# Fused attention and feed-forward kernel: other slots for the loads and turns of the tenth head pair

## The chip, the cores and the metric

The kernel runs on one core of one Trainium2 chip. The metric is the device time of one execution in microseconds (us), lower is better. The kernel before took 505.3 us, the median of 3 runs (504.86, 505.3 and 510.37).

An engine here is one of the core's instruction streams: PE (matrix products), PEld (PE's weight loads, which overlap PE), DVE (vector work), ACT (functions such as exp and tanh), POOL (general work), SP (issues transfers). Each works through its own list in order. ACT and SP also issue the DMA transfers of this kernel.

## The reference

There are 8 batches of 8 heads, sequence 576, head dimension 64. For every head, scores are formed, all that lie more than tau below the row's maximum are dropped, and the rest goes through a softmax; then a feed-forward layer with g = h - tanh(h) works on the 4608 rows of 512:

```
scores = scale * np.matmul(q, k.transpose(0, 1, 3, 2))
thresh = np.max(scores, axis=-1, keepdims=True) - tau
scores = np.where(scores >= thresh, scores, -1000000000.0)
scores = scores - np.max(scores, axis=-1, keepdims=True)
attn = np.exp(scores)
attn = attn / (np.sum(attn, axis=-1, keepdims=True) + 1e-09)
out = np.matmul(attn, v)
...
h = x @ w_in
g = h - np.tanh(h)
return (g @ w_out).astype(np.float32)
```

## The kernel before

**Tiles and slots.** Two heads make a pair; there are 32 pairs, numbered from 0, so that the tenth is pair 9. A pair has nine tiles of 128 query rows (four for each head, and one that holds the last 64 rows of both), 288 tiles in all. One loop runs over slots, one tile per slot. In slot s it issues, in this order: the scores of tile s+8 (PE, L401 and L410, reduced to a maximum by DVE in L420), the thresholding of tile s+5 (ACT, L447, which writes z), the feed-forward work that is due (PE L579 and L605, ACT L592, DVE L598), the exponentials (ACT L483, from the transposed z), the product with v of tile s-2 (PE L506, L513, L524), and at the end of the slot the steps that a plan has for it. After these come casts of the feed-forward weights (POOL, L731) and loads of further pieces of them (SP, L739, up to slot 53), at slots that two lists give.

**Who transposes z.** From pair 6 on, z is turned by a DMA transpose that SP issues (L454, zT), one for two tiles; before that PE turns it. Exponentials of two tiles are then one activation, in every second slot.

**What a pair needs before its scores.** Pair p's first scores are issued at slot 9p-8, which the code calls `first`: 73 for pair 9, 64 for pair 8, 82 for pair 10. For the pairs from 8 on (`DUAL`) eleven steps lead up to that, each with a lead d: the step is issued at the end of slot first-d.

- `k0`, `q0`, `q1`, `v0`, `v1`: loads of raw float32 data, issued by ACT (L175). k comes in one transfer of 288 KB, q in one of 256 KB and one of 32 KB, v in two, of 128 KB and 160 KB.
- `ks`, `qs`, `vs`: POOL splits k and q into a high and a low float16 half (L228, L231, L232; three passes each) and casts v to bfloat16 into one of four vb buffers (L261, L265, L266).
- `kt`, `qt`: SP issues a DMA transpose of the split k or q (L315), which gives kT and qT. For k of pair 8 PE does it.
- `kw`: POOL copies kT with its two halves exchanged (L337), which gives kS.

Raw and split data have two buffers per kind, kT, kS and qT three. `FIRST_LATER` has leads of their own for pairs 8 and 9, `LATER` has those of the later pairs, by even and odd number; pair 9's in the kernel before are the same as `LATER[1]`. The order of the list matters for steps of one slot alone. Within one slot, a pair with a lower number goes first. Since each engine takes its instructions in order, a lead sets both the time from which a step may run and what stands ahead of it in ACT's, POOL's or SP's queue.

Of the kernel before, what the change touches and what calls it, by code (L numbers as in the profile page):

```python
# [18 lines left out]
def kernel(  # L19
# [713 lines left out]
    def w_load(piece):  # L733
# [6 lines left out]
        else:  # L740
# [35 lines left out]
            ("kw", 3),  # L776
        ),
        9: (
            ("kt", 10), ("qt", 6), ("k0", 18), ("q0", 14), ("v0", 15),
            ("q1", 13), ("v1", 12), ("ks", 11), ("qs", 8), ("vs", 6),  # L780
            ("kw", 5),
        ),
    }
    for p in range(DUAL, NPAIR):
# [176 lines left out]
```

## Time and profile before

| what | value |
|---|---|
| median of 3 runs | 505.3 us |
| the profiled execution | 511.62 us, its span 509.7 us |
| PE busy | 484.8 us (95% of the span) |
| ACT busy | 431.7 us (85%) |
| DVE busy | 400.2 us (79%) |
| POOL busy | 291.4 us (57%) |
| transfers issued by SP | 75.1% of 16 DMA engines over the span |
| transfers issued by ACT | 16.1% |
| zT, issue to landing | median 4.7 us |
| kT, qT, issue to landing | median 5.2 and 4.3 us |
| k load issued by ACT, issue to landing | median 4.2 us |

The page of the profile describes one execution, which was 6.3 us longer than the median. Its second part cuts the span into 40 equal slices of about 12.7 us and gives a digit, in tenths, for each engine's busy share, for the clock granted to PE and for the DMA engines' share. An answer by stages gives the same for chosen stretches. A timeline lists instructions with start, duration and, in brackets, the idle time of the engine before them with what ended it. The time that a DMA issue takes on its queue is not the time that its data takes to land.

In this execution pair 9's loads went out at 88.87 us (k), 92.65 (v0), 97.67 (q0, and q1 behind it) and 100.77 (v1).

### The profile page before, as it was taken

What the parts mean: (1) busy time and instruction counts of PE and PEld (TensorE: products, weight loads), DVE (VectorE), ACT (ScalarE), POOL (GpSimd) and SP (SyncE); (2) the same over time, 40 slices, a digit from 0 to 9 for tenths busy, and PEclk for the clock granted to TensorE, in tenths of its full rate; (3) what the DMA queues carried; (4) which work ended last, traced back from release to release, by engine and by line L of the source; (5) the groups of instructions that cost most, each with busy time, mean ns of one, the idle gap of its engine ahead of it and who ended that gap; (6) DMA issues with size and microseconds to landing.
All of it is one profiled execution on the core that took longest, in us unless ns stands there. A gap on an engine that the chain in (4) does not pass through costs nothing.

```text
span 509.7 us, 12184 instructions
## 1 busy us (share of the span) xinstructions
PE 484.8 (95%) x4283; PEld 270.9 (53%) x4345; DVE 400.2 (79%) x1150; ACT 431.7 (85%) x617; POOL 291.4 (57%) x390
## 2 busy tenths in 40 slices
PE   8999899889999989999999999999998999999997
PEld 4666566445555545555555555555554555544444
DVE  5899978878889879988898789889886887544440
ACT  5999998889999889999999999899979999533430
POOL 8999999886765375757675666569456700000000
PEclk9999999989999999999999999999999999999999
DMA  7852658999999999999999999999999986311013
GB/s 206 262 155 89 195 190 220 159 225 214 231 217 245 192 254 209 238 241 242 242 195 221 261 238 225 207 242 240 213 191 258 187 144 115 87 41 42 23 41 82
DMA packets 233341, 95.32 MB, mean 187 GB/s; under 512 B 203968, under 2 KB 222656, under 8 KB 233280
## 3 DMA queue, kind: packets, MB, share of 16 engines
q1 hardware_dynamic: 212336, 72.87, 75.1%
q10 hardware_dynamic: 20944, 21.67, 16.1%
q8 instruction: 34, 0.56, 0.5%
q14 instruction: 27, 0.22, 0.2%
HBM read 36.70 MB, written 9.44 MB: 91 GB/s over the span
## 4 chain that ended last, share of the span: by engine, by line
PE 57%; POOL 12%; DMA 9%; issue 7%; ACT 7%; DVE 5%; ACTq 1%; SPq 0%; POOLq 0%; DVEq 0%
PE psY L605 18%; PE psH L579 14%; PE psS L410 13%; DMA zT<-z 6%; PE psO L513 3%; POOL kS L337 3%; PE psHt L579 3%; ACT pT L483 3%; DMA vraw<-in_v_dram 3%; ACT z L447 2%; DVE g L598 2%; POOL qhl L232 2%; DVE sc L420 2%; PE psS L401 2%; ACTq L175 1%
## 5 line engine op out<-in xcount | busy, mean ns | idle before, releaser
L420 DVE TENSOR_SCALAR_CACHE_REDUCE sc<-psS 128x576 f32<-128x576 f32 x288 | 213.5, 752 | 27.1 <-PE psS L410 12.9
L447 ACT ACTIVATE z<-sc,nb 128x576 bf16<-128x576 f32 x288 | 216.1, 770 | 8.0 <-DVE nb L432 5.7
L483 ACT ACTIVATE pT<-zT 128x1152 f16<-128x1152 bf16 x117 | 135.2, 1155 | 12.3 <-DMA zT<-z 10.6
L605 PE MATMUL psY<-w_out_sb,g 128*128 128x512 bf16 (+1 forms) x564 | 140.8, 373 | 1.6 <-issue 0.2
L579 PE MATMUL psH<-xT,w_in_sb 128*128 128x512 bf16 x448 | 119.4, 381 | 5.1 <-issue 2.0
L337 POOL COPY kS<-kT 64x1152 f16<-64x1152 f16 x62 | 70.8, 1142 | 86.3 <-DMA kT<-khl 72.7
L598 DVE SCALAR_TENSOR_TENSOR g<-th,psH 128x512 bf16<-128x512 f32 x128 | 87.6, 685 | 33.6 <-ACT th L592 32.9
L410 PE MATMUL psS<-kT,qT 128*128 128x512 f16 (+1 forms) x512 | 104.7, 286 | 4.1 <-DVE sc L420 1.9
L410 PE MATMUL psS<-kS,qT 128*128 128x512 f16 (+1 forms) x512 | 105.1, 287 | 0.0
L410 PEld LDWEIGHTS <-qT 128*128 128x128 f16 x1024 | 72.5, 98 | 59.0 <-issue 3.8
L592 ACT ACTIVATE th<-psH 128x512 f32<-128x512 f32 x128 | 74.6, 583 | 21.4 <-PE psH L579 21.4
L605 PEld LDWEIGHTS <-g 128*128 128x128 bf16 x592 | 51.1, 98 | 54.6 <-DVE g L598 0.4
L579 PEld LDWEIGHTS <-w_in_sb 128*128 128x128 bf16 x576 | 49.4, 98 | 57.4 <-issue 6.3
L513 PE MATMUL psO<-vb,pT 128*128 128x65 bf16 x1024 | 53.3, 194 | 0.0
L513 PEld LDWEIGHTS <-pT 128*128 128x128 f16 x1024 | 44.2, 98 | 9.6
L232 POOL TENSOR_TENSOR qhl<-qraw,qhl 128x576 f16<-128x576 f32 x31 | 39.7, 1281 | 2.6
L232 POOL TENSOR_TENSOR khl<-kraw,khl 128x576 f16<-128x576 f32 x31 | 39.7, 1280 | 2.7
L475 ACT ACTIVATE pT<-psZ 128x512 f16<-128x512 bf16 (+1 forms) x54 | 35.1, 654 | 2.4 <-PE psZ L466 2.1
L506 PE MATMUL psO<-vb,pT 128*128 128x130 bf16 x128 | 28.2, 220 | 3.7 <-ACT pT L483 3.6
L617 DVE COPY yo<-psY 128x512 f32<-128x512 f32 (+1 forms) x31 | 21.1, 680 | 13.1 <-PE psY L605 12.4
L539 DVE TENSOR_TENSOR osb<-psO,rc 128x256 bf16<-128x256 f32 x64 | 27.2, 424 | 2.2
L228 POOL TENSOR_SCALAR qraw<-qraw 128x576 f32<-128x576 f32 x31 | 20.8, 671 | 11.1 <-DMA qraw<-in_q_dram 10.8
(77 smaller groups left out, 452.1 us busy)
## 6 DMA issues: line engine op xcount, KB each, us to landing
out_dram<-yo SPq DMA_DIRECT2D x32, 256.0 KB, 3.8
kraw<-in_k_dram ACTq DMA_DIRECT2D x24, 288.0 KB, 4.2
qraw<-in_q_dram ACTq DMA_DIRECT2D x24, 256.0 KB, 4.3
wt<-in_moe_w_in_dram SPq DMA_DIRECT2D x8, 512.0 KB, 4.6
wt<-in_moe_w_out_dram SPq DMA_DIRECT2D x8, 512.0 KB, 3.9
vraw<-in_v_dram ACTq DMA_DIRECT2D x24, 160.0 KB, 4.3
vraw<-in_v_dram ACTq DMA_DIRECT2D x24, 128.0 KB, 3.8
vraw<-in_v_dram SPq DMA_DIRECT2D x8, 256.0 KB, 3.6
```

Of the source, the lines that this page charges most:

```text
L232: nc.gpsimd.tensor_tensor(out=hl[:, :, 1, :], in0=x, in1=hl[:, :, 0, :], op=ALU.subtract)
L337: nc.gpsimd.tensor_copy(out=o, in_=i)
L410: nc.tensor.matmul(out=ps[:, dst], lhsT=lhs, rhs=cols(p, kk, hh), start=(n == 0), stop=(n == 1),)
L420: nc.vector.tensor_scalar(out=sc, in0=ps[:, lo : lo + S], scalar1=SC, scalar2=None, op0=ALU.mult, op1=ALU.max, accum_out=mx[:, c : c + 1],)
L447: nc.scalar.activation(out=z, in_=sc, func=ACT.Prelu, bias=nb, scale=1.0, alpha=STEEP)
L475: nc.scalar.activation(out=pt[:, off * P : (off + n) * P], in_=ps[:, 0 : n * P], func=ACT.Exp)
L483: nc.scalar.activation(out=pt[:, 0 : n * P], in_=zts.pop(i)[:, 0:n, :], func=ACT.Exp)
L513: nc.tensor.matmul(out=po[:, t - 1 + ab, :], lhsT=pt[:, blk * P : (blk + 1) * P], rhs=vb[:, hh, c, :], start=False, stop=(n == 7), skip_gr ...
L579: nc.tensor.matmul(out=ps, lhsT=w_in_sb[:, c, n * P : (n + 1) * P], rhs=xs[m][:, c, :] if m < B else xR[:, c, :, :], start=(c == 0), stop= ...
L592: nc.scalar.activation(out=th, in_=ps, func=ACT.Tanh)
L598: nc.vector.scalar_tensor_tensor(out=gs[m][:, n, :], in0=th, scalar=-1.0, in1=ps, op0=ALU.mult, op1=ALU.add,)
L605: nc.tensor.matmul(out=ps, lhsT=gs[m][:, n, ms * P : (ms + 1) * P], rhs=w_out_sb[:, n, cols], start=(n == 0), stop=(n == DF_C - 1),)
```

## The change

Pair 9 gets another list. Nine of its eleven steps move; nothing is added or removed, and no other pair is touched.

| step | queue | slot before | slot after |
|---|---|---|---|
| k0 | ACT | 55 | 52 |
| q0 | ACT | 59 | 55 |
| q1 | ACT | 60 | 56 |
| v0 | ACT | 58 | 57 |
| v1 | ACT | 61 | 59 |
| ks | POOL | 62 | 60 |
| qs | POOL | 65 | 62 |
| kt | SP | 63 | 63 |
| qt | SP | 67 | 65 |
| kw | POOL | 68 | 66 |
| vs | POOL | 67 | 67 |

Pair 8's own steps lie at 46 (k0), 49 (q0, q1), 50 (v0), 52 (v1), 54 (qs), 56 (ks), 57 (kt), 58 (vs) and 59 (qt); pair 10's begin with k0 at 64.

```diff
         9: (
-            ("kt", 10), ("qt", 6), ("k0", 18), ("q0", 14), ("v0", 15),
-            ("q1", 13), ("v1", 12), ("ks", 11), ("qs", 8), ("vs", 6),
-            ("kw", 5),
+            ("k0", 21), ("v1", 14), ("q0", 18), ("v0", 16), ("qs", 11),
+            ("q1", 17), ("qt", 8), ("ks", 13), ("vs", 6), ("kt", 10),
+            ("kw", 7),
         ),
```

## The prediction

> **What bounds the kernel now.** I read the page first: span, busy shares, slices.
>
> ```profile
> span 509.7 us, 12184 instructions
> ...
> PE 484.8 (95%) x4283; PEld 270.9 (53%) x4345; DVE 400.2 (79%) x1150; ACT 431.7 (85%) x617; POOL 291.4 (57%) x390
> ...
> PEclk9999999989999999999999999999999999999999
> DMA  7852658999999999999999999999999986311013
> ```
>
> PE is busy 95% of the span, so a moved load is worth only what PE stands still for it. Two things stand out: the DMA share goes to 9 from the eighth slice on (about 89 us), where the zT transposes have begun, and the clock row has one 8, in the ninth slice (102 to 115 us). Pair 9 (the tenth) is loaded just before. So next comes the table by stage, core 0 (the stretch and its length; busy us and count of PE, PEld, DVE, ACT, POOL; then clock, DMA share, GB/s):
>
> ```profile
> 84.00:88.00 4.00, 3.88 (x43) 2.49 (x44) 3.28 (x11) 3.90 (x8) 3.73 (x7) 1.00 1.01 241
> 88.00:92.00 4.00, 3.60 (x39) 1.93 (x37) 3.92 (x13) 3.57 (x6) 3.85 (x5) 1.00 1.31 201
> 92.00:96.00 4.00, 3.95 (x49) 2.66 (x48) 4.00 (x13) 3.84 (x6) 2.08 (x3) 1.00 1.09 99
> 96.00:100.00 4.00, 2.73 (x27) 1.41 (x25) 3.02 (x10) 2.33 (x3) 3.76 (x6) 1.00 1.46 186
> 100.00:104.00 4.00, 1.69 (x17) 0.72 (x15) 2.27 (x7) 3.88 (x6) 3.85 (x5) 1.00 1.06 225
> ...
> 104.00:108.00 4.00, 3.77 (x17) 1.88 (x19) 1.76 (x4) 3.41 (x6) 3.75 (x7) 0.57 1.36 235
> ```
>
> At 92 to 96 the DMA engines are full and yet move 99 GB/s, where the stages around move 186 to 241. Right after it PE falls to 2.73 and 1.69 of 4 us. The timeline of PE, ACT and SP says why (start, us, instruction; in brackets the idle time before it and what ended it):
>
> ```profile
> 98.88 0.23 PE L506 MATMUL psO<-vb,pT 128*128 128x130 bf16 x1 [1.27 <-ACT pT L483]
> 101.98 0.23 PE L506 MATMUL psO<-vb,pT 128*128 128x130 bf16 x1 [0.77 <-ACT pT L483]
> 104.02 0.42 PE L410 MATMUL psS<-kT,qT 128*128 128x512 f16 x2 [1.55 <-DMA qT<-qhl]
> ```
> ```profile
> 92.65 0.61 ACTq L175 DMA_DIRECT2D vraw<-in_v_dram  x1
> 97.67 1.16 ACT L483 ACTIVATE pT<-zT 128x1152 f16<-128x1152 bf16 x1 [1.83 <-DMA zT<-z]
> 97.67 1.06 ACTq L175 DMA_DIRECT2D qraw<-in_q_dram  x2
> ```
> ```profile
> 87.87 9.58 SPq L454 DMA_TRANSPOSE zT<-z  x3
> 97.63 2.04 SPq L315 DMA_TRANSPOSE qT<-qhl  x1
> ```
>
> The exponentials wait for a zT, PE for the exponentials, and last for pair 8's qT, issued behind three zTs and beside pair 9's two q loads at 97.67. The chain of work that ended last runs through the same place (start, us, what):
>
> ```profile
> 91.28 9.46 DMA zT<-z
> 100.74 0.02 issue
> 100.76 0.01 ACT pT L483
> 100.77 4.70 DMA vraw<-in_v_dram
> ```
>  The three waits are 1.27+0.77+1.55 = 3.6 us. At clock 0.57 a busy 3.77 us does the work of 0.57×3.77, so 1.6 us more goes. The stretch costs **5.2 us**.
>
> **What the Trainium skill says.** "DMA: Bandwidth & Descriptors", section "Issuing engines are not separate DMA queues": transfers started by ACT and SP run on the same 16 engines and interleave. The trace agrees: pair 9's k load (ACT, 88.87) took 8.6 us to land, the slowest of the two zTs (SP) issued from 87.5 to 92 took 9.8, against a zT median of 4.7. "Perfetto Trace Analysis", section on HWDGE DMA instructions: an issue's duration is lock wait plus descriptor generation, and the data movement is outside it. The trace agrees: zT issues at 84.76, 87.87 and 94.14 took 1.26, 2.01 and 3.31 us, their landings more. "TensorE: Matmul & The Clock Gate", Part 1: idle PE drops to half clock, in windows of 3.4 us. Here 0.57 over 4 us fits one such window (1-0.5×3.4/4 = 0.575).
>
> **The change part by part.** No instruction or byte is added; eleven steps keep their kind, nine change slot. One slot is about 1.4 us here (nine tiles in 13.4).
>
> *k0 from slot 55 to 52 (ACT queue).* It will go out behind v1 of pair 8, which is in slot 52 already (84.62, 0.65 us), so at about 85.3 instead of 88.87. Its 0.35 us issue then is in the open: the activation over it is 0.60 long, v1 alone uses that up, so ACT is later by up to 0.4. ACT had a hole of 0.43 at 88.3 (z waits for th) that takes it: 0. Buffer: pair 7's k was split by POOL at 74.74 to 77.5; no wait. Its 288 KB are 1.4 us of DMA time at the 206 GB/s of 86 to 92, so the zT at 84.76 (landed 89.17, used at 92.30: cover 3.1) lands up to 1.4 later: 0.
>
> *q0 59 to 55, q1 60 to 56, v0 58 to 57, v1 61 to 59 (ACT queue).* q0 takes k0's place at 88.9 (256 KB for 288), q1 (32 KB) follows at about 91, v0 moves from 92.65 to about 92.3, v1 from 100.77 to 97.67. Issues of 0.40, 0.59, 0.61, 0.61 us lie under activations of 0.57 to 1.16: 0. The two q loads leave 97.67, where they share the engines with qT of pair 8: 288 KB or 1.4 us of DMA time go from there, v1's 160 KB come. The zTs at 87.87 and 91.28 get q0, q1 for k0: bytes equal within 10%, smaller rows. The zT at 87.87 was wanted at 95.84, when ACT fell idle: 8.0 us after issue, against 4.4 for the zT before it, a cover of 3.6.
>
> *ks 62 to 60, qs 65 to 62 (POOL queue).* The three-pass splits are 2.7 us each (0.67+0.66+1.28 with gaps). ks passes one weight cast (1.04), so starts at 99.35 instead of 100.36; qs 103.06 instead of 104.07. Its loads land by 97. The cast of slot 60 ends at about 103.1 instead of 100.4; the first psY matmul is at 115.3: cover 12. 0.
>
> *kt stays at 63, qt 67 to 65 (SP queue).* qt now stands ahead of the zT of slot 66, behind that of slot 64, whose issue ends at 108.7; qhl is ready at 105.8. The zT of slot 66 goes from 109.05 to about 110.0, lands at 113.8 instead of 112.76; its exponential is at 116.84. Cover 3: 0. qT of pair 9 comes 1.8 earlier, wanted by PE at 117.25: 0.
>
> *kw 68 to 66, past vs (POOL queue).* POOL's swap waits for kT (issued 104.07, landed 109.66, as SP holds kt at its place); vs (1.3 us) now waits behind it, to 113.4 instead of 108.07. Pair 9's vb is first read in slot 85, after 134: cover 20. Pair 10's ks, qs start 1.3 later (113.4, 116.1); its kt goes out at 116.81 and needs ks by then (116.1): cover 0.7, and if that went, the swap (120.6) would slip against a first use at 130: 0.
>
> So all moved issues cost nothing under these covers; what is left is **the stretch of 5.2 us**. Bounds: all of it goes, if the 99 GB/s stage needs k0 beside the zTs of 87.87 and 91.28; none, if q0 in its place does the same; and as much again is lost (+5.2) in an execution without it, if k0 and v1 together do it one zT earlier.
>
> What is in the runs that set the median? The profiled execution took 511.62 us (span 509.7 and 1.9 around it), the median is 505.3, 6.3 less; the runs are 504.86, 505.3 and 510.37. Taking the stretch out of the profiled time gives 506.4, near the median. I take it that the median's execution has most of it not: zTs land in the ordinary 4.4. Then the third zT issue ends at 94.14+1.3 = 95.4, qT of pair 8 goes at 95.6 and lands 4.3 later (page median of qT) at 99.9; PE, without 2.04 of earlier waits, wants it at 102.47-2.04 = 100.4. That cover is 0.5, and one pressed landing (1.4 of DMA time by the q loads) makes a wait of 0.9. The change removes the q loads from beside it: between 0 and 1.4; I take 0.7. **505.3-0.7 = 504.6**. For an execution with the stretch: 511.6-5.2 = 506.4.
>
> **The rivals.** *A, forecast*: covers hold, only the thin cover at qT matters: 503.9 to 505.3, with run spread 503 to 506.5. For: every cover above. Against: the median may carry the stretch. Chance 0.52. *B, faster*: all executions carry the stretch, so all lose it: 505.3-5.2 = 500.1. For: the load that landed in 8.6 us is the very one moved. Against: 506.4 would be what is left of the profile, and pairs 10 to 31 also have k0 beside transposes, and later PE stands still for over 1 us only near 180 and 380. Chance 0.14, nearly all of it over 1%. *C, slower*: at slot 52, k0 follows the zT of 84.76 by 0.55 us with v1 (160 KB) and a 512 KB weight piece in flight. k loads at 263.35 and 370.77, out 0.6 and 0.55 us after a zT, landed in 6.6 and 6.8. If zTs at 84.76 and 87.87 then land over 7.5 us after issue (the covers of 7.5 and 8.0 decide), PE pays 3.6 waiting and a half-clock window, 5.2: 510.5. Chance 0.19. *D, it does not matter*: the stretch comes as before, only with q0: the time stays at 505.3 to 505.8. Chance 0.15; it falls within 1%.
>
> **Numbers.** A measurement of this kernel tells about 1% (5 us) from no change. Within 1%: A 0.52, D 0.15 and the part of B and C that is milder, 0.05: 0.72. Slower 0.17, faster 0.11. The range reaches to B and C's centres, 500.1 and 510.5, and leaves out about half of each, under 0.2: 500.0 to 510.6. A alone spans 503 to 506.5.
>
> **What would show it.** Right: k landing in under 6 us from 85.3, no stage at 88 to 100 below 150 GB/s, qT of pair 8 landing before PE asks, no 8 in the clock row. If C: waits for zT already at 92 to 96. If the thin cover is nothing: qT's wait gone and the time still 505.3. Wrong altogether: a wait of PE or POOL at 116 to 135 on pair 9's or 10's tiles, which would show one of the covers false.

## The result, and the profile after

The changed kernel takes 512.28 us (median of 17 runs, 509.41 to 519.67), the kernel before in the same comparison 507.56 (17 runs, 503.42 to 514.73). The ratio is 1.0107, 95% interval 1.0079 to 1.0136: slower by about 1%. The ratios here leave out the runs that took over 1.5% more than the fastest of the same kernel, the medians do not, and since this kernel scatters by more than that the two can differ by half a per cent. The median of before is 2.3 us above the 505.3 of the three runs that the prediction had.

The profiled execution of the changed kernel took 513.09 us. From the first and second part of its page:

```profile
span 511.2 us, 12245 instructions
...
PE 490.9 (96%) x4345; PEld 271.1 (53%) x4345; DVE 399.2 (78%) x1150; ACT 431.4 (84%) x617; POOL 291.8 (57%) x390
...
PEclk9999999999999999999999999999999999999999
DMA  7852657999999999999999999999999876311013
```

The 8 in the clock row is gone. (The profile of before, and every other of a whole kernel here, records 62 matrix products fewer, x4283 against x4345, so the busy times of PE over the span are not comparable.) The table by stage of the changed kernel, with the same columns as in the prediction:

```profile
88.00:92.00 4.00, 3.70 (x39) 1.89 (x36) 3.64 (x12) 4.00 (x7) 3.85 (x5) 1.00 1.11 279
92.00:96.00 4.00, 3.93 (x48) 2.54 (x47) 4.00 (x12) 3.83 (x6) 1.79 (x2) 1.00 1.23 162
96.00:100.00 4.00, 3.62 (x35) 1.85 (x32) 3.84 (x12) 3.66 (x6) 3.70 (x7) 1.00 1.26 225
100.00:104.00 4.00, 3.47 (x32) 1.93 (x31) 2.63 (x9) 4.00 (x6) 3.85 (x5) 1.00 1.23 237
104.00:108.00 4.00, 3.17 (x36) 1.92 (x34) 3.78 (x11) 3.89 (x7) 3.12 (x4) 1.00 1.29 139
```

Nothing here falls to 99 GB/s, and PE is busy for 3.17 us of 4 or more, where before had a stage with 1.69. Read against the first profile alone, this stretch is better: the score reduction (DVE, L420) of tile 72, pair 8's first, starts at 102.7 us, where it was 105.0. (Below, a tile's start is the start of its score reduction.) A second profile of the kernel before settles which of the two is the ordinary case. Its rows, same columns:

```profile
92.00:96.00 4.00, 3.95 (x49) 2.66 (x48) 4.00 (x13) 4.00 (x7) 2.08 (x3) 1.00 1.08 256
96.00:100.00 4.00, 3.62 (x30) 1.81 (x28) 3.96 (x13) 3.81 (x6) 3.77 (x6) 1.00 1.17 196
100.00:104.00 4.00, 3.68 (x32) 2.06 (x32) 2.46 (x8) 4.00 (x7) 3.85 (x5) 1.00 1.14 152
```

256 GB/s at 92 to 96, full clock, and tile 72 at 101.8. So the stretch is not in every execution; of the eight profiles with pair 9's k and q at their old places or later (below), the first alone has it. Against the second profile the changed kernel is late at each step: tile 72 (pair 8's first) by 0.9 us, tile 81 (pair 9's) by 1.8, tile 90 (pair 10's) by 3.0.

### The profile page after: what moved, and what is told of

It reads as the page before. It is cut to its first block, busy times and chain, and to the rows that moved or that the text cites. A ratio compares the mean times of both kernels' runs of the same rounds, so it can differ in the third digit from the quotient of the medians.

```text
span 511.2 us, 12245 instructions
## 1 busy us (share of the span) xinstructions
PE 490.9 (96%) x4345; PEld 271.1 (53%) x4345; DVE 399.2 (78%) x1150; ACT 431.4 (84%) x617; POOL 291.8 (57%) x390
## 4 chain that ended last, share of the span: by engine, by line
PE 57%; DMA 11%; POOL 11%; ACT 9%; issue 5%; DVE 3%; ACTq 2%; SPq 0%; POOLq 0%
PE psY L605 18%; PE psH L579 15%; PE psS L410 13%; DMA zT<-z 10%; ACT z L447 4%; ACT pT L483 4%; PE psO L513 3%; PE psHt L579 3%; POOL kS L337 2%; ACT th L592 2%; PE psS L401 2%; ACTq L175 2%; DVE g L598 1%; PE psO L524 1%; DVE sc L420 1%
## 5 line engine op out<-in xcount | busy, mean ns | idle before, releaser
L420 DVE TENSOR_SCALAR_CACHE_REDUCE sc<-psS 128x576 f32<-128x576 f32 x288 | 213.2, 751 | 22.3 <-PE psS L410 12.5
L483 ACT ACTIVATE pT<-zT 128x1152 f16<-128x1152 bf16 x117 | 135.2, 1156 | 15.2 <-DMA zT<-z 13.3
L605 PE MATMUL psY<-w_out_sb,g 128*128 128x512 bf16 (+1 forms) x592 | 145.7, 373 | 0.0
L579 PE MATMUL psH<-xT,w_in_sb 128*128 128x512 bf16 x480 | 123.3, 379 | 2.0 <-DVE g L598 1.8
L410 PE MATMUL psS<-kT,qT 128*128 128x512 f16 (+1 forms) x512 | 104.4, 285 | 4.5 <-DVE sc L420 3.1
L617 DVE COPY yo<-psY 128x512 f32<-128x512 f32 (+1 forms) x31 | 21.0, 678 | 12.8 <-PE psY L605 12.4
```

Source lines behind the costliest of these rows:

```text
L410: nc.tensor.matmul(out=ps[:, dst], lhsT=lhs, rhs=cols(p, kk, hh), start=(n == 0), stop=(n == 1),)
L420: nc.vector.tensor_scalar(out=sc, in0=ps[:, lo : lo + S], scalar1=SC, scalar2=None, op0=ALU.mult, op1=ALU.max, accum_out=mx[:, c : c + 1],)
L483: nc.scalar.activation(out=pt[:, 0 : n * P], in_=zts.pop(i)[:, 0:n, :], func=ACT.Exp)
L579: nc.tensor.matmul(out=ps, lhsT=w_in_sb[:, c, n * P : (n + 1) * P], rhs=xs[m][:, c, :] if m < B else xR[:, c, :, :], start=(c == 0), stop= ...
L605: nc.tensor.matmul(out=ps, lhsT=gs[m][:, n, ms * P : (ms + 1) * P], rhs=w_out_sb[:, n, cols], start=(n == 0), stop=(n == DF_C - 1),)
```

## The experiments

Theory L: the earlier loads press the zT transposes of slots 52 to 56. Theory T: the other moved steps cost it, above all qt ahead of the zT of slot 66; it is narrowed below to theory K, kw ahead of vs on POOL. Where nothing else is said an edit is on the list for pair 9, and the diffs show the changed entries alone.

**The kernel before once more.**

> The kernel before once more, for a second profile of it and for the size of a difference that is none. Both theories: ratio 1.000, within 0.4%. Theory L (the earlier loads press the zT transposes of slots 52 to 56) expects zT of these slots landing in about 4.4 to 6 us here and PE idle under 2 us at 96 to 116, if the stretch of 5.2 us of the first profile is not in every execution; if it is, L cannot explain the loss, since the change took that stretch away.

508.92 us against 508.42, ratio 0.9991 (0.9947 to 1.0035). zT of slots 52, 54 and 56 landed in 5.2, 6.8 and 4.4 us, near the 4.4 to 6 expected; the stretch is not there.

**One half each.** Loads alone:

```diff
-("k0", 18), ("q0", 14), ("v0", 15), ("q1", 13), ("v1", 12)
+("k0", 21), ("q0", 18), ("v0", 16), ("q1", 17), ("v1", 14)
```

> Only the five loads of pair 9 moved (k0, q0, q1, v0, v1 at slots 52, 55, 56, 57, 59), the splits, turns and the swap as before. Theory L, that the earlier loads make zT late, expects nearly the whole loss: ratio 1.007 to 1.012, and zT of slots 52 to 56 landing in over 7 us. Theory T, that the turn of q standing ahead of the zT of slot 66 and the earlier POOL steps cost it, expects 0.997 to 1.002.

511.93 against 508.42, ratio 1.0022 (0.9986 to 1.0058). The landings came as theory L has them, 9.8, 11.0 and 10.7 us, tile 72 at 106.0, in an execution of 515.06 us; the ratio did not reach the loss that it expected. The medians lie 3.5 us apart and the ratio says 1.1, so time leaves open what this half costs. The other half alone:

```diff
-("ks", 11), ("qs", 8), ("qt", 6), ("kw", 5)
+("ks", 13), ("qs", 11), ("qt", 8), ("kw", 7)
```

> Only ks, qs, qt and kw moved (slots 60, 62, 65, 66), the loads as before; POOL may wait about 1 us for q, whose small load goes out in slot 60. Theory T expects 1.007 to 1.012, with the zT of slot 66 issued over 1.5 us later than in the kernel before. Theory L expects 0.998 to 1.003.

510.45 against 508.42, ratio 1.0048 (1.0022 to 1.0073). zT landings at slots 52 to 56 are ordinary (5.4, 7.0, 4.6). The zT of slot 66 went out 2.6 us later than in the second profile of before, as theory T has it, but the ratio did not reach its 1.007. So the second half alone costs time, under half of the whole loss, and neither theory alone is right; that the loads have the rest follows from the difference, not from their own ratio. The turn of q put back in the changed kernel:

```diff
-("qt", 8)
+("qt", 6)
```

> The changed kernel with the turn of q alone put back to slot 67, behind the zT of slot 66. Theory T expects the loss gone: 0.998 to 1.003. Theory L expects it to stay: 1.007 to 1.012.

512.48 against 508.42, ratio 1.0073 (1.0043 to 1.0104): most of the loss stays, so qt ahead of the zT of slot 66 is not the heart of the second half. The traces showed something else: in the kernels with kw moved, ACT stood idle before the exponential of slot 77 (2.16 us with the second half alone, 1.15 in the changed kernel, 0.72 here, 0.0 in both profiles of before). This became theory K.

**Single steps.** kw alone, kw back, k0 alone, q alone:

```diff
-("kw", 5)                  kw alone, on the kernel before
+("kw", 7)
...
-("kw", 7)                  kw back, on the changed kernel
+("kw", 5)
...
-("k0", 18)                 k0 alone
+("k0", 21)
...
-("q0", 14), ("q1", 13)     q alone
+("q0", 18), ("q1", 17)
```

> The kernel before with kw alone moved, from slot 68 to 66, ahead of vs on POOL's queue. Theory K (the swap waits on POOL for kT, everything behind it is late, the split of pair 10's k ends later, its turn stands at the head of SP's queue until then and the zT of slot 72 stands behind it) expects the split of pair 10's k to end over 1.2 us later against the first score of pair 9 than before, the turn of pair 10's k to go out at its end, an idle ACT of 1 to 2 us before the exponential of slot 77, and a ratio of 1.002 to 1.006. The rival, that only pair 9's loads cost time, expects 1.000 within 0.3% and no such idle time.

510.45 against 508.96, ratio 1.0014 (0.9983 to 1.0044): under the 1.002 to 1.006 of theory K and not told from none by time, though the idle time came, 2.44 us.

> The changed kernel with kw put back to slot 68, behind vs. Theory K expects the idle time before the exponential of slot 77 gone and a ratio of 1.003 to 1.007, some 0.4% under the 1.0107 of the whole change; the rest is left to the loads. The rival, that only the loads cost time, expects 1.008 to 1.013.

511.05 against 508.96, ratio 1.0080 (1.0046 to 1.0115), over what K expected and at the lower end of what its rival, that only the loads cost time, expected; the idle time before slot 77 is gone as K expected.

> The kernel before with k0 alone moved, from slot 55 to 52. Theory L in the form that k behind v1 is enough expects zT of slot 52 landing in 6.5 us or more (4.4 and 5.2 before), an ACT hole of about 0.8 us at 86 us, the zT of slot 54 issued some 0.7 us later, and a ratio of 1.002 to 1.005. In the form that the q loads are needed besides, zT of slots 54 and 56 land as before and the ratio is 1.000 within 0.3%.

508.95 against 508.96, ratio 1.0021 (0.9987 to 1.0055), which fits either form. zT of slot 52 landed in 5.9, short of 6.5, and ACT's hole at 86 us was 1.02.

> The kernel before with q0 and q1 alone moved, from slots 59 and 60 to 55 and 56, so that k and q go out together in slot 55. Theory L in the form that the q loads press the zT of slots 54 and 56 expects both landing in over 7 us (6.8 and 4.4 in the second profile of the kernel before), the zT of slot 52 as before, and 1.002 to 1.006. In the form that k behind v1 does it: 1.000 within 0.3%.

507.53 against 508.96, ratio 0.9994 (0.9969 to 1.0020), no loss, although in the profiled execution the zTs of slots 52 to 56 landed in 7.1, 10.3 and 10.4 and tile 72 started at 104.9. How often that happens a single execution doesn't say, and the q loads alone are not shown to cost anything.

**The kernel ended after slot 111.** Whole runs scatter by 11 us, so single steps drown. Ended early, the kernel keeps all that lies around pair 9's loads; it leaves out the attention of pairs 12 to 31 and all feed-forward work after that slot:

```diff
-    for s in range(-AHEAD, NTILE + LAG + 3):
+    for s in range(-AHEAD, 112):
...
+    stage, todo = NMB, []
```

> The kernel before, ended after slot 111: pairs 12 to 31 are not attended, all feed-forward work after that slot is left out, and most of the output is not written. All that lies around pair 9's loads stays as it is, and what 20 later pairs add to the time falls away. About 160 us; the spread of its runs should be well under the 12 us of the whole kernel.

> The changed kernel, ended after slot 111 in the same way. If the loss of about 5 us arises at pairs 8 to 11, where zT lands late, this is 2.5 to 5 us over the cut kernel before. If it arises later, because all later transfers meet each other at other times, it is under 1 us.

> Only the five loads of pair 9 moved, ended after slot 111. Theory L (earlier loads make the zT of slots 52 to 56 late) expects over half of the cut loss, 1.5 to 3 us over the cut kernel before. The rival, that the splits, turns and swap cost it, expects under 0.5 us.

> Only ks, qs, qt and kw moved, ended after slot 111. Theory K (the swap ahead of vs, and the wait before the exponential of slot 77) expects 1 to 2.5 us over the cut kernel before. The rival, that loads alone cost time, expects under 0.5 us.

| ended after slot 111 | median of 5 or 6 runs, us | lowest to highest |
|---|---|---|
| before | 180.42 | 178.13 to 181.51 |
| changed | 183.51 | 180.33 to 184.80 |
| loads alone | 182.01 | 177.47 to 182.15 |
| second half alone | 182.37 | 179.49 to 183.35 |

The medians put 3.1 us of the loss in this part, about the amount by which tile 90 is late in the profiles (130.4 and 130.6, against 127.3 and 127.4). The runs are few: the ratios to the whole kernel, 0.3572 against 0.3540, make it 1.6 us, with intervals that overlap. By the medians each half is within what its own theory expected (1.6 us for the loads, 2.0 for the second half), but the ranges of both overlap that of before. The rest of the loss comes later. The landings of the three zTs of slots 52 to 56, by tile, first the ended kernel before, then the ended changed one:

```profile
L454 SPq DMA_TRANSPOSE zT<-z x3: 1248/1284/1448, 84.8 to 91.3; - x3
...
DMA to landing us min/median/max: 4.0/5.4/6.4
```
```profile
L454 SPq DMA_TRANSPOSE zT<-z x3: 1248/2268/4746, 85.2 to 92.1; - x3
...
DMA to landing us min/median/max: 8.1/9.7/9.9
```

The slowest landing before is 1.7 us shorter than the fastest after. Issues grow with them, 4.7 us for one, and what SP has to issue next waits behind that.

Then the single steps, ended in the same way, in a further comparison:

> kw alone moved to slot 66, ahead of vs, ended after slot 111. Theory K, that this order is the whole second half, expects 1.5 to 2.5 us over the cut kernel before (180.0), with an idle ACT of about 2 us before the exponential of slot 77. If ks, qs or qt are needed besides, under 0.7.

180.74 (177.22 to 184.13), 0.3 over the median of before: not the 1.5 us expected in time, though ACT was idle for 1.4 us before the exponential of slot 77 and for 1.2 before that of 81, and tile 90 came at 129.4.

> The changed kernel with kw back behind vs, ended after slot 111. Theory K expects what the loads alone cost, 180.7 to 181.7, and no idle time before the exponential of slot 77. If the loss of the two halves does not come from kw, it stays at 183.

182.38 (180.11 to 183.98), between the 181.7 of theory K and the 183 of its rival; no idle time before slot 77; tile 90 at 128.9.

> k0 alone moved to slot 52, ended after slot 111. If k behind v1 is enough for theory L: 180.7 to 182, zT of slot 52 landing in 6.5 us or more. If the q loads are needed besides: 180.0 to 180.5.

182.08 (180.40 to 182.24). In this execution k behind v1 was enough: zT landed in 8.7, 9.0 and 8.9, tile 72 at 104.4. In the whole kernel above it was not (5.9, 6.0 and 6.4).

> k0, q0 and q1 moved to slots 52, 55 and 56, v as before, ended after slot 111. Theory L with q: zT of slots 52, 54 and 56 landing in over 7 us each, 181 to 182.5. If v, one and two slots sooner, is what matters: 180.0 to 180.5.

With k0, q0 and q1 moved: 181.13 (180.14 to 182.50), zT landings 7.8, 10.4 and 11.0. The times of these four overlap; they do not rank the steps.

**Other traffic out of the way.** In the changed kernel, ended after slot 111, the last two weight pieces, 512 KB each, were loaded later (an entry of these lists is a slot plus 8, so 58 is slot 50):

```diff
-    load_when = [..., 52, 55, 58, 61]
-    cast_when = [..., 62, 65, 68, 71]
+    load_when = [..., 52, 55, 70, 73]
+    cast_when = [..., 62, 65, 77, 80]
```

> The changed kernel, ended after slot 111, with the last two weight pieces (512 KB each) loaded in slots 62 and 65 and cast in 69 and 72, where they were loaded in 50 and 53 and cast in 60 and 63. Theory L expects zT of slots 52 and 54 landing in about 5 to 6 us instead of 8.1 and 9.7, no wait of ACT before slot 63, and the loss of the loads gone, 180.5 to 182, if the pieces do no harm at their new place. If it is not a matter of bytes in flight, the landings stay over 7 and the time at 183.

The landings of the same three zTs, with pair 9's loads where the change puts them:

```profile
L454 SPq DMA_TRANSPOSE zT<-z x3: 1274/1292/2299, 84.7 to 91.6; - x3
...
DMA to landing us min/median/max: 4.2/4.3/4.4
```

From 8.1 to 9.9 down to 4.4 and less, and tile 72 at 102.1: in these two executions the early loads made the zTs late only together with the pieces. SP issues the pieces and the zTs alike, so this run does not say whether the bytes in flight or the place on SP's queue count; that k, which ACT issues, makes them late too speaks for the bytes. But the pieces did harm where they went (the zT of slot 64 landed in 6.7, ACT waited 2.3 us before slot 71 and 1.8 before 77), and the kernel took 184.43 us, over the 180.5 to 182 expected and over the 183.51 it was to beat.

**k the other way.** On the kernel before, whole:

```diff
-("k0", 18)
+("k0", 15)
```

> The kernel before, whole, with k0 moved the other way, from slot 55 to 58. Theory L expects the zT of slot 54 landing in about 5 us (6.8, 6.4 and 5.6 before) and a ratio of 0.994 to 1.000; POOL's split of k may wait for it, and if that holds kt up, the ratio is 1.000 to 1.004.

507.96 against 508.26, ratio 1.0028 (0.9999 to 1.0057). The zT of slot 54 landed in 5.1 us as expected, but pair 9's kT took 6.0 to land, POOL waited 1.1 us for it, and ACT was idle 1.9 before slot 77. No kernel here is shown to beat the kernel before.

## Why the prediction was wrong

The forecast was 504.6 us, no change; the time is 512.28, outside the range of 500.0 to 510.6, and the change costs where a small gain was forecast. 2.3 us of the 7.7 are the median of three runs that it stood on. The rest, point by point. (A slot is 1.5 us, 13.4 over nine, not 1.4; nothing rests on it.)

**The stretch and the median.** Right, as far as one execution shows: the second profile of before, of 507.69 us, does not have the stretch. Its size was off: the sum of waits and clock made 5.2 us, but tile 90 is 3.4 us later in the first profile than in the second (130.7 and 127.3) and the span 3.9 longer. The larger harm was that the covers were read in that one execution, as the points below show.

**"cover of 3.6" for the zT of slot 54.** This is the step that failed first. It took 4.4 us as the ordinary landing, from the zT before it. In seven of the eight profiles of kernels that leave pair 9's k and q no earlier than slot 55 and 59, this zT landed in 5.1 to 7.0 us (9.8 in the first), so against 8.0 us the cover is 1.0 to 2.9. And equal bytes did not leave it equal: k went out while v1 of pair 8 and a weight piece were in flight. The prediction let it cost the zT of slot 52 at most 1.4 us of DMA time, in a cover of 3.1. That zT landed in 4.3 to 5.5 us in those eight profiles, and in 5.9 to 9.8, median 7.6, in the ten with k in slot 52 and the weight pieces in place; in nine of the ten the zTs of slots 54 and 56 are late as well, with 7.4 to 11.0. Over those eight profiles the median start of tile 72 is 101.8 us; over the eleven with k or q moved and the weight pieces in place it is 104.3. Part of these 2.5 us is made up later: in the five of these eleven in which pair 10's kT goes out in time (below), tile 90 is late by 1.0 to 3.5 us, in four of them by 1.6 or less.

**"ACT had a hole of 0.43 at 88.3 (z waits for th) that takes it: 0".** Wrong in size. ACT in the changed kernel:

```profile
84.69 0.59 ACT L475 ACTIVATE pT<-psZ 128x512 f16<-128x512 bf16 x1
84.69 0.65 ACTq L175 DMA_DIRECT2D vraw<-in_v_dram  x1
85.43 0.61 ACTq L175 DMA_DIRECT2D kraw<-in_k_dram  x1
86.09 0.77 ACT L447 ACTIVATE z<-sc,nb 128x576 bf16<-128x576 f32 x1 [0.81 <-DVE sc L420]
```

The issue of k took 0.61 us, not 0.35, and ACT stood open for 0.81 us (DVE is named, but ACT's queue was issuing until 86.04). The z that was at 85.33 in the first profile came at 86.09 and the zT of slot 54 went out at 88.63 instead of 87.87: 0.76 us later, with the landing to follow.

**"0.7" gained at qT of pair 8.** Not there to be gained: in the second profile of before qT landed at 100.96 and PE, busy until then, began at 101.00. The change brought a wait instead: with SP held by zT issues of 1.87, 3.11 and 1.96 us, qT went out at 96.84 and PE waited 0.53 us for it.

**"cover 0.7, and if that went, the swap (120.6) would slip against a first use at 130: 0" for kw.** This step failed too, in two ways. The cover was read in the first profile, where SP and PE were 3.4 us late and POOL's split of pair 10's k only 1.6:

```profile
113.61 1.28 POOL L232 TENSOR_TENSOR khl<-kraw,khl 128x576 f16<-128x576 f32 x1
...
116.81 1.30 SPq L315 DMA_TRANSPOSE kT<-khl  x1
```

The split ended at 114.89, 1.9 us ahead of its turn. In the second profile, below, it ended at 113.32, 0.1 ahead, so there was no room for a move of over 1 us. And the prediction asked only what a late turn does to POOL's swap, not what stands behind that turn on SP. POOL, SP and the exponential of slot 77, first in the second profile of before, then with kw alone moved:

```profile
107.78 0.29 POOL L266 CAST vb<-vraw 64x128 bf16<-64x128 f32 x1
108.14 2.33 POOL L337 COPY kS<-kT 64x1152 f16<-64x1152 f16 x2
112.04 1.28 POOL L232 TENSOR_TENSOR khl<-kraw,khl 128x576 f16<-128x576 f32 x1
...
109.87 3.38 SPq L454 DMA_TRANSPOSE zT<-z  x2
113.41 1.48 SPq L315 DMA_TRANSPOSE kT<-khl  x1
115.29 4.14 SPq L454 DMA_TRANSPOSE zT<-z  x2
...
121.07 1.16 ACT L483 ACTIVATE pT<-zT 128x1152 f16<-128x1152 bf16 x1
```
```profile
107.94 2.32 POOL L337 COPY kS<-kT 64x1152 f16<-64x1152 f16 x2 [1.09 <-DMA kT<-khl]
113.21 1.28 POOL L232 TENSOR_TENSOR khl<-kraw,khl 128x576 f16<-128x576 f32 x1
...
110.04 3.23 SPq L454 DMA_TRANSPOSE zT<-z  x2
114.51 1.29 SPq L315 DMA_TRANSPOSE kT<-khl  x1
115.90 4.49 SPq L454 DMA_TRANSPOSE zT<-z  x2
...
123.64 1.16 ACT L483 ACTIVATE pT<-zT 128x1152 f16<-128x1152 bf16 x1 [2.44 <-DMA zT<-z]
```

In the kernel before, vs fills the wait for pair 9's kT, which landed at 107.6, and the swap starts right behind it. With kw first POOL stands still for 1.09 us, pair 10's k is split 1.17 us later, and SP, free at 113.27 in place of 113.25, holds its turn until that split ends at 114.49. The zT of slot 72 stood behind it: it went out 0.6 us later and landed in 7.7 us instead of 5.5. Why it landed more slowly no run separates; the turn was in flight beside it. The profiles agree on what a late turn goes with. In the eight where pair 10's kT goes out 1.6 us ahead of the reduction of tile 81, tiles 81 to 90 take 12.3 us, every time. In the ten where it goes out at most 0.8 us ahead, or after it, they take 12.8 to 16.5; seven of the eight profiles with kw moved are among these ten, and three of the twelve with kw in place. In the two between (1.1 and 1.3 us ahead; q alone, and the changed kernel ended early) they take 12.3 and 12.4, so this part is not in every execution of the change. The changed kernel's own lines:

```profile
111.14 2.33 POOL L337 COPY kS<-kT 64x1152 f16<-64x1152 f16 x2 [3.87 <-PE psS L410]
116.43 1.28 POOL L232 TENSOR_TENSOR khl<-kraw,khl 128x576 f16<-128x576 f32 x1
...
117.74 1.39 SPq L315 DMA_TRANSPOSE kT<-khl  x1
...
124.16 1.16 ACT L483 ACTIVATE pT<-zT 128x1152 f16<-128x1152 bf16 x1 [1.15 <-DMA zT<-z]
```

Here kT of pair 9, issued at 102.76, took 8.2 us to land, and POOL waited 3.87 us (the page names PE, but 110.99 is when kT landed). kw is not the only way into this: with k0 alone in the whole kernel, and with k0 later, kw in its place, a late kT of pair 9 ate the same margin. Timed, kw alone is not told from none; the chain is shown in the traces, its share of the median is not.

**qt ahead of the zT of slot 66: "0".** Not settled. The issue took 2.98 us instead of 1.3, and that zT went out at 110.85 instead of about 110.0. The kernel with qt put back has a ratio of 1.0073, the changed one 1.0107, and their intervals overlap. Between tiles 72 and 81 the changed kernel loses 0.9 us more: ACT is idle for 1.14 us before the exponential of slot 69, whose zT, of slot 64, took 6.9 us to land where it took 4.2 in the second profile of before. No run says which of the moved steps did that.

**The rivals.** C was the right one: its place (k behind v1 in slot 52), its sign, and about its deciding point, landings over 7.5 us and covers of 7.5 and 8.0. In the profile of the changed kernel the two zTs landed in 7.3 and 7.9 us and ACT waited 0.34 us for the second; ended early, in 8.1 and 9.7 us, with waits of 0.2 and 2.1. Its way to the size was another: not 3.6 us of PE standing and a half-clock window, since the clock stayed at 1.00, but a later start of pair 8 and then pair 10's share. That its centre, 510.5, is near the 512.28 is luck. C was held against covers that were each counted as if the others were untouched. Of the signs for A, the clock row and the GB/s came as named, but k landed in 6.5 us, not under 6, and qT after PE asked for it.

**Open: the later part.** The difference of the medians is 4.7 us, of which the ended kernels have 1.6 to 3.1. The profiles of the whole kernels, one execution each, show where the rest comes. Against the second profile of before the changed kernel is 2.5 us late at pair 11, still 2.5 at pair 15, 7.9 at pair 22 and 5.4 at the end; from pair 15 to pair 22 ACT waited 8.3 us for zTs, against 1.5. All four whole kernels with the five loads moved (changed, loads alone, qt back, kw back) gain 2.9 to 5.0 us of lateness between pair 11 and the end, and ACT waits for zTs for 13.3 to 17.6 us over the span. The six others beside the second profile of before gain at most 0.5, and these six and it wait for 7.6 to 11.5. So the five loads together seem to have the later part too. Why loads of pair 9 are felt at pairs 15 to 22, whose own steps are untouched, stays open.

## What to carry to other kernels

A load that is moved earlier can be paid for by the transfers that are in flight at its new place; take the cover of each of those from several profiles of the same transfer, not from its neighbour, since here 3.6 us of cover were 1 to 3. Follow a moved step through every queue in turn: a late step on POOL made a transpose late that held the head of SP's queue, and the harm was done to the transfer behind it. And where a profile shows an accident, take a second before reading any cover from the first: here the engines were late by different amounts, and 1.9 us of room for the split were 0.1.

## What the runs showed of the hardware

The same transpose of 128x1152 values landed in 3.5 to 11.0 us (slots 52 to 56, 20 profiles), and its issue on SP took 1.25 to 5.9 us, in the same places of kernels that differ in the steps of one pair or in two weight loads. The DMA engines could be full (shares of 1.09 and 1.08) and move 99 GB/s in one execution and 256 in another at the same place of the same kernel. A k load's issue on ACT took 0.33 to 0.43 us, and 0.55 to 0.82 in all eleven cases where it stood straight behind another load's. In the first profile of before, the clock granted to PE was 0.50 from 104.32 to 107.73 us, after 3.42 us in which PE was busy for 1.10 us, its longest single idle time being 1.55.
